# The last token group of a fused attention and feed-forward kernel: 256 tokens, computed and stored token-major

## The chip, the cores and the metric

The kernel runs on one core of one Trainium2 chip. The metric is the device time of one execution in microseconds. A core has five engines with a queue of instructions each: TensorE (PE, with its weight loads as PEld) multiplies matrices into the accumulator memory PSUM; ScalarE (ACT) evaluates functions such as tanh; VectorE (DVE) does elementwise work, reductions and 32x32 block transposes; GpSimd (POOL) and SyncE (SP) do little here but issue DMAs. Each queue is worked off in order. An instruction that needs another engine's result waits on a semaphore, and so does everything behind it in its queue. DMAs between the on-chip memory SBUF and device memory are issued from a queue (here SP's, ACT's or POOL's) and carried out by 16 DMA engines.

## The reference

A polynomial attention without softmax gives x, and a two-layer block with the function h - tanh(h) follows. Shapes: batch 4, heads 4, sequence 1088, head dimension 32; so x has 4352 rows (tokens) of 128.

```python
def phi(x):
    a = np.einsum('rd,bhsd->bhsr', S1, x)          # r = 8
    b = np.einsum('rd,bhsd->bhsr', S2, x)
    return np.einsum('bhsi,bhsj->bhsij', a, b).reshape(*x.shape[:-1], r * r)
q_p, k_p = (phi(q), phi(k))
kv = np.einsum('bhsf,bhsd->bhfd', k_p, v)
z = np.sum(k_p, axis=2)
num = np.einsum('bhsf,bhfd->bhsd', q_p, kv)
den = np.einsum('bhsf,bhf->bhs', q_p, z)[..., None] + 1e-06
attn = num / den
x = np.ascontiguousarray(attn.transpose(0, 2, 1, 3)).reshape(4352, 128)
h = x @ w_in                                        # 128 -> 2048
g = h - np.tanh(h)
out = (g @ w_out).astype(np.float32)                # 2048 -> 128
```

## The kernel before

The kernel is written as a list of operations. Each names its engine or engines, what it reads and writes, an estimated cost and a sort key (`P.add`, L102); `schedule` (L139) places them on the engines by these estimates, `sync` (L268) puts in the semaphores, and `emit` (L316) writes each engine's queue. Buffers come from pools (`_Pool`, `_Val`): an operation that takes a buffer again waits for those that used it last.

Attention leaves its result as `xT` in bfloat16, with the 128 features on the partitions and the tokens as columns. The columns of one batch are ordered by `s = t * 34 + c` with c slow and t fast (NC = 34 blocks of 32 columns): 32 neighbouring columns of `xT` are 32 tokens that lie 34 rows apart in the output, and four blocks of 32 are four neighbouring rows at each t.

The feed-forward part, `ffn(gi, c0, n_)` from L966, works on groups of columns; `GCOLS` (L19) has their sizes, and the last two of the ten have 512 and 192. For each group:

- Sixteen matmuls (L986) make h: for each slice jb of 128 of the 2048 hidden units, the slice of w_in is stationary and the group's columns of xT are moving. They go to PSUM banks of the pool `bank_h` (tiles psh and psa).
- ACT's tanh (L991) takes a unit of m slices at a time from PSUM to a bfloat16 tile `th`; in the last three groups (`gi >= WIDE`, 7) m is 2, or 4 for a group of at most 256 columns; in the first group it is 2, otherwise 1.
- Eighteen matmuls (L1001, L1005) accumulate the output in one bank of the pool `bank_o` (pso or psa): sixteen with a slice of w_out stationary and th moving, and two with a precomputed product of the two weight matrices (`wch` and its rounding rest `wcl`), which supply the linear part h @ w_out. tanh is taken of -h, so that all add up. The result has the 128 outputs on the partitions and the tokens as columns.
- One DVE transpose of 32x32 blocks (L1010) brings it to a tile `ot`: then each group of 32 partitions holds 32 of the 128 outputs, with t on the partitions and (c, m) along the row.
- Four stores (L1020), one for each group of 32 outputs, write `ot` to the output in rows of 32 floats (128 bytes). A group that crosses a batch boundary has eight. They are all issued from SP, except that in the last group two of the four go to ACT's queue. `ot` has three buffers.

At the very end POOL waits for all stores (L1069).

The order around the change: PE's queue interleaves the h matmuls of a unit with the output matmuls of an earlier unit, and the h matmuls of the last group begin while the group before is still being accumulated. On ACT nothing but tanh stands behind the last copies of attention (L378), until the two stores at the end.

Of the kernel before, what the change touches and what calls it, by code (L numbers as in the profile page):

```python
# [4 lines left out]
B, H, S, D = 4, 4, 1088, 32  # L5
R = 8
DM = 128
DFF = 2048
NJB = DFF // 128
NC = 34  # L10
# [5 lines left out]
AF = mybir.ActivationFunctionType  # L16
AX = mybir.AxisListType

GCOLS = [256, 384, 448] + [512] * 6 + [192]  # L19
T_FIRST = 12500.0  # L20
VLAND = [9900.0, 10500.0, 6800.0, 8000.0]
QLAND = [8000.0, 10200.0]
# [306 lines left out]
def _vp(n):  # L329
    return {"vector": (n / 0.96 + 76.0, 158.0)}  # L330


def _a(n):
    return {"scalar": (n * 0.8333 + 50.0, 175.0)}
# [10 lines left out]
def _pe(ns):  # L345
    return {"tensor": (ns, 215.0)}


def bass_polysketch_attn__then__act_tanh_shrink_kernel(
# [10 lines left out]
    P = _Prog()  # L360
    uid = [0]

    def sb(name, shape, dtype=FP32):
        uid[0] += 1
        return nc.alloc_sbuf_tensor(f"{name}_{uid[0]}", shape, dtype).ap()

    def ps(name, n=1):
        uid[0] += 1
        return nc.alloc_psum_tensor(f"{name}_{uid[0]}", [128, n * 512], FP32).ap()
# [4 lines left out]
    def pool(name, n, shape, dtype=FP32):  # L374
        return _Pool([sb(name, shape, dtype) for _ in range(n)])

    def copy(e, name, o, i):
        return e.copy(o, i) if name == "scalar" else e.tensor_copy(o, i)  # L378

    def slices(pl, parts):  # L380
        pl.slots = [[t[:, c:c + w], 0.0, [], (t, c, w)] for (t, c, w) in parts]
        return pl
# [3 lines left out]
    bank_h = slices(_Pool([], True), [(psh, i * 512, 512) for i in range(4)] + [(psa, i * 512, 512) for i in range(2)])  # L386
    bank_o = _Pool([ps("pso"), psa[:, 1024:1536]], True)
# [29 lines left out]
    ot_p = pool("ot", 3, [128, 512])  # L417
    xT = sb("xT", [128, B * S], BF16)
# [12 lines left out]
    wob = sb("wo", [128, NJB, DM], BF16)  # L431
# [3 lines left out]
    woh = [_Val(ap=wob[:, i * 8:(i + 1) * 8, :]) for i in range(2)]  # L435
# [7 lines left out]
                                          start=True, stop=True) for w in (128, 256)], zop, bank_o)  # L443

    def pool_op(fn, r=(), w=(), n=100, key=-50000.0):
        return P.add(_g(n), fn, r=r, w=w, key=key)
# [3 lines left out]
        out=ident.ap[:, :], in_=ident.ap[:, :], pattern=[[-1, 128]], compare_op=ALU.not_equal,  # L450
# [3 lines left out]
        out=mask4.ap[:, :], in_=ident.ap.rearrange("p (q h j) -> p h q j", q=4, h=4), op=ALU.add, axis=AX.XY),  # L454
        r=[ident], w=[mask4], key=-90000)
    P.add(_v(128), lambda e, n: e.tensor_reduce(
        out=mask1.ap[:, :], in_=ident.ap.rearrange("p (h d) -> p h d", h=H), op=ALU.add, axis=AX.X),
        r=[ident], w=[mask1], key=-92000)
    P.add(_v(128), lambda e, n: e.tensor_reduce(
        out=mask2.ap[:, :], in_=ident.ap.rearrange("p (a e d) -> p e a d", a=2, e=2), op=ALU.add, axis=AX.XY),  # L460
        r=[ident], w=[mask2], key=-91000)
    for pl, f, val in ((kT_p, lambda a: a[:, 1088:1152], 0.0), 
                       (m_p, lambda a: a[:, :, 8:9], 1e-6)):
        for i, s_ in enumerate(pl.slots):
            o = pool_op(lambda e, n, a=f(s_[0]), val=val: e.memset(a, val), n=64, key=-49000)
# [82 lines left out]
    gstart = []  # L548
    t = T_FIRST
    for i, gc in enumerate(GCOLS):  # L550
        gstart.append(t)
        t += PERIOD * gc / 512.0

    def col_time(c):
        a = 0
        for i, gc in enumerate(GCOLS):
            if c < a + gc:
# [6 lines left out]
        r=[sqv], w=[stt], key=-85000)  # L564
    P.add(_g(64, 2.2), lambda e, n: e.tensor_tensor(
        out=wq3s.ap.rearrange("p h (x i) -> p h x i", i=8),
        in0=tt[:, None, :, :].to_broadcast([128, H, 2, 8]),
        in1=mask1.ap[:, :, None, None].to_broadcast([128, H, 2, 8]), op=ALU.mult),
        r=[stt, mask1], w=[wq3s], key=-47000)
    P.add(_v(32), lambda e, n: e.tensor_tensor(  # L570
        out=wab.ap.rearrange("p (x e i) -> p x e i", e=2, x=2),
        in0=tt[:, :, None, :].to_broadcast([128, 2, 2, 8]),
        in1=mask2.ap[:, None, :, None].to_broadcast([128, 2, 2, 8]), op=ALU.mult),
        r=[stt, mask2], w=[wab], key=-85000)
    for w, z in zip(wqc, wqs):
# [3 lines left out]
            r=[stt], w=[w], n=16, key=-48000)  # L579
    P.add(_g(128, 2.2), lambda e, n: e.tensor_tensor(  # L580
        out=s2r.ap.rearrange("p (h d) -> p h d", h=H),
        in0=sq[:, 1, None, :].to_broadcast([128, H, 32]),
        in1=mask4.ap[:, :, None].to_broadcast([128, H, 32]), op=ALU.mult),
        r=[sqv, mask4], w=[s2r], key=-70000)

    xvals = []
    seq = [0]
# [348 lines left out]
    def weights():  # L936
# [19 lines left out]
        for jb in range(16):  # L956
# [6 lines left out]
        P.add(_vp(128), lambda e, n: e.tensor_tensor(out=wcl.ap[:, :], in0=wc.ap[:, 0:128], in1=wch.ap[:, :],  # L963
                                                     op=ALU.subtract), r=[wc, wch], w=[wcl], key=-60000.0, name="wcl")

    def ffn(gi, c0, n_):  # L966
        t0 = gstart[gi]
        step = PERIOD / 16 * n_ / 512
        xs = [xv for (a, z, xv) in xvals if a < c0 + n_ and z > c0]
        xt = xT[:, c0:c0 + n_]  # L970
        ov = _Val(bank_o)
        ths = []
        wide = gi >= WIDE
        m = 4 if wide and n_ <= 256 else 2 if wide or n_ <= 256 else 1
        per = 2 if n_ <= 256 else 1
        pitch = 256 if n_ <= 256 else 512
        for j0 in range(0, NJB, m):
            hv = _Val(bank_h, n=m // per)
            th = _Val(th_p, n=-(-m * n_ // 512))
            for j in range(m):  # L980
                jb = j0 + j
                ths.append((th, j * n_))

                def mm(e, n, jb=jb, j=j, hv=hv):
                    c = j % per * pitch
                    return e.matmul(hv.bank(j // per)[:, c:c + n_], wib[:, jb * 128:(jb + 1) * 128], xt, start=True, stop=True)  # L986
                P.add(_pe(n_ / 2.4 + 2.6), mm, r=[wih[jb // 4]] + xs, w=[hv], key=t0 + jb * step, mode="128x128", name=f"h{gi}.{jb}")

            def tanh(e, n, hv=hv, th=th):
                i = hv.ap.rearrange("p (j x) -> p j x", x=pitch)[:, :, 0:n_]  # L990
                return e.activation(out=th.ap[:, 0:m * n_].rearrange("p (j x) -> p j x", x=n_), in_=i, func=AF.Tanh, scale=-1.0)  # L991
            P.add({"scalar": (m * n_ * 0.8333 + 64.0, 175.0)}, tanh,
                  r=[hv], w=[th], key=t0 + (j0 + m - 1) * step, name=f"th{gi}.{j0}")
        seq = [("t", j) for j in range(NJB)]
        at = 15 if gi < 2 else 8
        seq[at:at] = [("c", wch), ("c", wcl)]
        prev = None
        for i, (kind, x) in enumerate(seq):
            st, sp_ = i == 0, i == len(seq) - 1
            if kind == "t":  # L1000
                fn = lambda e, n, x=x, st=st, sp_=sp_: e.matmul(  # L1001
                    ov.ap[:, 0:n_], wob[:, x, :], ths[x][0].ap[:, ths[x][1]:ths[x][1] + n_], start=st, stop=sp_)
                rd = [woh[x // 8], ths[x][0]]
            else:
                fn = lambda e, n, x=x, st=st, sp_=sp_: e.matmul(  # L1005
                    ov.ap[:, 0:n_], x.ap[:, :], xt, start=st, stop=sp_)
                rd = [x] + xs
            prev = P.add(_pe(n_ / 2.4 + 2.6), fn, r=rd, w=[ov], key=t0 + i * step + 1500, chain=prev, mode="128x128", name=f"o{gi}.{i}")
        ot = _Val(ot_p)
        P.add(_vp(n_), lambda e, n: e.transpose(ot.ap[:, 0:n_], ov.ap[:, 0:n_]), r=[ov], w=[ot], key=-60000, name=f"ot{gi}")  # L1010
        cb = c0 // 32
        ce = (c0 + n_) // 32
        while cb < ce:
            b = cb // NC
            cn = min(ce, (b + 1) * NC)
            off = cb * 32 - c0
            for qd in range(4):
                dst = out[b * S:(b + 1) * S, :].rearrange("(t c) m -> t c m", c=NC)[:, cb - b * NC:cn - b * NC, qd * 32:(qd + 1) * 32]
                last = gi == len(GCOLS) - 1
                P.add({"scalar" if last and qd % 2 else "sync": (450.0, 0.0)}, lambda e, n, qd=qd, dst=dst, off=off, w_=(cn - cb) * 32: e.dma_start(  # L1020
                    out=dst, in_=ot.ap[qd * 32:(qd + 1) * 32, off:off + w_].rearrange("p (c m) -> p c m", m=32)),
                    r=[ot], key=t0, dma=(cn - cb) * 32 * 128 / 150.0)
            cb = cn
# [3 lines left out]
    st = {}  # L1027
    for name in ORDER.split():
        b = int(name[1])
# [6 lines left out]
    c = 0  # L1036
    for gi, gc in enumerate(GCOLS):
        ffn(gi, c, gc)
        c += gc
# [75 lines left out]
```

## Time and profile before

| | us |
|---|---|
| median of 13 runs | 108.51 |
| lowest and highest of them | 108.0 and 109.85 |
| the profiled execution, its own time | 108.58 |
| its span in the trace | 106.6 |
| ACT busy in the span | 83.5 (78%) |
| DVE busy | 67.3 (63%) |
| tanh (L991) for 10 groups: 114 and 10 instructions, by the tile they read | 63.2 and 8.6 |
| mean duration of a tanh of 1024 columns from psh (11 of them) | 1.064 |
| mean duration of a tanh of 768 columns from psh (3) | 0.811 |
| output stores: 46 issued from SP, 2 from ACT | |

The span runs from the first to the last instruction in the trace; the execution's own time is 2.0 us longer. The mean durations of matmuls and tanhs include their pipeline's latency, so consecutive ones overlap, and sums of them are no times; the distance between two starts is the cost of one in a row. A view of the profile gives for each row a start or a count, a length, the engine (PE, PEld, DVE, ACT; SPq and ACTq are DMA issues from that queue), the line of the kernel and the tiles as out<-in, and in brackets the idle time before it with what ended it.

### The profile page before, as it was taken

How to read it: one execution, taken by the hardware profiler on the slowest of the kernel's cores; microseconds unless marked ns; L12 is line 12 of the kernel's file. 1: busy time of each engine (PE TensorE's matmuls, PEld its weight loads, DVE VectorE, ACT ScalarE, POOL GpSimd, SP SyncE). 2: the span in 40 equal slices, each digit the busy share in tenths (PEclk: the TensorE clock that was granted, in tenths of full speed). 3: DMA queues.
4: the chain of work that ended last, by engine and by line, in shares of the span. 5: the costliest groups of instructions: out<-in, count | busy, mean ns of one | idle time of the engine just before them, and what ended most of it. 6: DMA issues, size and time to landing. Idle time of an engine off the chain costs nothing.

```text
span 106.6 us, 3421 instructions
## 1 busy us (share of the span) xinstructions
PE 99.2 (93%) x1455; PEld 51.2 (48%) x1455; DVE 67.3 (63%) x114; ACT 83.5 (78%) x174; POOL 5.0 (5%) x23
## 2 busy tenths in 40 slices
PE   5977799899999999999999999999999999999960
PEld 4544688476654356543346343344533444334730
DVE  4569949997965999999999980999420020020210
ACT  0400499997758888788898979999989999999950
POOL 5410320000000000000000000000000000000000
PEclk9999999999999999999999999999999999999997
DMA  2989799966169654015940240033003214014153
GB/s 52 231 249 249 237 118 273 281 188 158 60 152 259 174 104 74 0 22 122 251 122 0 39 66 0 0 53 52 0 3 53 43 31 74 0 16 71 15 79 56
DMA packets 26430, 10.73 MB, mean 101 GB/s; under 512 B 21152, under 2 KB 24240, under 8 KB 26416
## 3 DMA queue, kind: packets, MB, share of 16 engines
q1 hardware_dynamic: 22368, 8.69, 35.5%
q0 software_dynamic: 2112, 0.54, 5.1%
q10 hardware_dynamic: 1936, 1.29, 4.7%
q8 instruction: 11, 0.18, 0.7%
q14 instruction: 3, 0.02, 0.1%
HBM read 8.81 MB, written 2.23 MB: 104 GB/s over the span
## 4 chain that ended last, share of the span: by engine, by line
PE 40%; ACT 31%; DVE 13%; DMA 10%; issue 2%; SPq 1%; DVEq 0%
ACT th L991 27%; PE pso L1001 12%; PE psh L986 9%; DMA vL<-in_v_dram 7%; PE psa L871 7%; DMA sq<-in_S_dram 3%; ACT xT L378 3%; DVE w L735 3%; PE psa L765 2%; DVE abc L812 2%; DVE qp L855 2%; PE psh L671 1%; DVE ot L1010 1%; PE pso L1005 1%; PE psa L804 1%
## 5 line engine op out<-in xcount | busy, mean ns | idle before, releaser
L991 ACT ACTIVATE th<-psh 128x512 bf16<-128x512 f32 (+4 forms) x114 | 63.2, 651 | 3.0 <-PE psh L986 2.8
L986 PE MATMUL psh<-xT,wi 128*128 128x512 bf16 (+4 forms) x142 | 44.0, 347 | 0.1
L1001 PE MATMUL pso<-th,wo 128*128 128x512 bf16 (+3 forms) x128 | 40.3, 358 | 0.3
L1001 PEld LDWEIGHTS pso<-th,wo 128*128 128x128 bf16 x128 | 11.7, 97 | 16.3 <-ACT th L991 4.3
L986 PEld LDWEIGHTS psh<-xT,wi 128*128 128x128 bf16 x142 | 13.4, 98 | 11.4 <-ACT th L991 1.1
L1010 DVE STREAM_TRANSPOSE ot<-pso 128x512 f32<-128x512 f32 (+3 forms) x8 | 5.2, 644 | 15.7 <-PE pso L1001 15.7
L860 DVE STREAM_TRANSPOSE qpT<-qp 128x768 f32<-128x768 f32 (+1 forms) x14 | 12.1, 861 | 0.4
L735 DVE TENSOR_TENSOR w<-abk 128x768 f32<-128x768 f32 (+2 forms) x12 | 11.0, 946 | 0.1
L855 DVE TENSOR_TENSOR qp<-ap,abc 128x768 f32<-128x768 f32 (+1 forms) x13 | 10.7, 825 | 0.1
L871 PE MATMUL psa<-qpT,kvb 32*32 32x128 f32 (+4 forms) x336 | 8.5, 309 | 0.2 <-issue 0.2
L991 ACT ACTIVATE th<-psa 128x1024 bf16<-128x1024 f32 (+2 forms) x10 | 8.6, 908 | 0.0
L442 PE MATMUL pso<-zz 128*128 128x256 bf16 (+1 forms) x41 | 7.4, 337 | 1.1 <-DVE zz L441 1.1
L871 PE MATMUL psh<-qpT,kvb 32*32 32x128 f32 (+4 forms) x112 | 8.5, 310 | 0.0
L1001 PE MATMUL psa<-th,wo 128*128 128x512 bf16 (+1 forms) x32 | 7.4, 314 | 0.3 <-ACT th L991 0.2
L871 PEld LDWEIGHTS psa<-qpT,kvb 32*32 32x32 f32 x336 | 5.1, 103 | 3.6 <-DVE qpT L860 1.2
L1010 DVE STREAM_TRANSPOSE ot<-psa 128x512 f32<-128x512 f32 (+1 forms) x2 | 1.1, 550 | 8.6 <-PE psa L1001 8.6
L442 PEld LDWEIGHTS pso<-zz 128*128 128x128 bf16 x41 | 4.5, 122 | 2.8 <-DVE zz L441 1.1
L986 PE MATMUL psa<-xT,wi 128*128 128x512 bf16 (+1 forms) x18 | 5.6, 349 | 0.0
L615 DVE STREAM_TRANSPOSE qT<-qL 128x576 f32<-128x576 f32 (+3 forms) x8 | 5.4, 706 | 0.0
L809 DVE STREAM_TRANSPOSE abc<-psh 128x288 f32<-128x288 f32 x3 | 1.4, 482 | 5.1 <-PE psh L804 5.0
L703 ACT ACT_TABLE_LOAD x1 | 1.3, 1283 | 4.2 <-issue 4.2
L1001 PEld LDWEIGHTS psa<-th,wo 128*128 128x128 bf16 x32 | 2.6, 97 | 3.6 <-ACT th L991 3.0
(87 smaller groups left out, 96.6 us busy)
## 6 DMA issues: line engine op xcount, KB each, us to landing
vL<-in_v_dram SPq DMA_DIRECT2D x11, 144.0 KB, 3.9
wif<-in_moe_w_in_dram SPq DMA_DIRECT2D x4, 256.0 KB, 6.0
out_dram<-ot SPq DMA_DIRECT2D x16, 64.0 KB, 2.0
kL<-in_k_dram SPq DMA_DIRECT2D x3, 288.0 KB, 3.2
qL<-in_q_dram SPq DMA_DIRECT2D x3, 288.0 KB, 3.8
kL<-in_k_dram SPq DMA_DIRECT2D x3, 256.0 KB, 3.9
qL<-in_q_dram SPq DMA_DIRECT2D x3, 256.0 KB, 3.9
wo<-in_moe_w_out_dram POOLq DMA_DIRECT2D x2, 256.0 KB, 5.7
```

Source lines behind the costliest of these rows:

```text
L378: return e.copy(o, i) if name == "scalar" else e.tensor_copy(o, i)
L442: filler = ([lambda e, n, w=w: e.matmul(bank_o.slots[0][0][:, 0:w], zz.ap[:, 0:128], zz.ap[:, 128:128 + w], start=True, stop=True) for w i ...
L615: P.add(_v((z - a) * 32), lambda e, n: e.transpose(qTs[b][:, a * 32:z * 32], val.ap), r=[val], w=tvs, key=nk(), name=f"qT{b}.{i}")
L735: P.add(_v(nx * 64), lambda e, n: e.tensor_tensor(out=wv.ap[:, 0:nx * 64].rearrange("p (x i j) -> p x i j", i=8, j=8), in0=abh(0)[:, :, :, ...
L765: i = e.matmul(bk[2].ap[h * 32:(h + 1) * 32, 0:64], vL[b][:, h, blk * 32:(blk + 1) * 32], wvs[b, p].ap[:, (bi * 4 + h) * 64:(bi * 4 + h + ...
L855: P.add(_v(cn * 256), lambda e, n, qp=qp, c0=c0, cn=cn: e.tensor_tensor(out=qp.ap[:, 0:cn * 256].rearrange("p (x i j) -> p x i j", i=8, j= ...
L860: P.add(_v(cn * 256), lambda e, n, qp=qp, o0=o0, cn=cn: e.transpose(qt.ap[:, o0 * 256:(o0 + cn) * 256], qp.ap[:, 0:cn * 256]), r=[qp], w=[ ...
L871: i = e.matmul(banks[g].ap[h * 32:(h + 1) * 32, 0:nb * 32], kvb.ap[g * 32:(g + 1) * 32, x, h * 32:(h + 1) * 32], qq[g * 32:(g + 1) * 32, 0 ...
L986: return e.matmul(hv.bank(j // per)[:, c:c + n_], wib[:, jb * 128:(jb + 1) * 128], xt, start=True, stop=True)
L991: return e.activation(out=th.ap[:, 0:m * n_].rearrange("p (j x) -> p j x", x=n_), in_=i, func=AF.Tanh, scale=-1.0)
L1001: fn = lambda e, n, x=x, st=st, sp_=sp_: e.matmul(ov.ap[:, 0:n_], wob[:, x, :], ths[x][0].ap[:, ths[x][1]:ths[x][1] + n_], start=st, stop=sp_)
L1010: P.add(_vp(n_), lambda e, n: e.transpose(ot.ap[:, 0:n_], ov.ap[:, 0:n_]), r=[ov], w=[ot], key=-60000, name=f"ot{gi}")
```

## The change

The last two groups become 448 and 256 instead of 512 and 192. The group of 256 is computed with the operands swapped: for each of its two tiles of 128 tokens, the tile's columns of th (or of xT) are stationary and the slice of w_out (or wch, wcl) is moving, so that the result has the tokens on the partitions and the 128 outputs along the row. Each tile has its own PSUM bank, one from `bank_o` and one from `bank_h`; the two are accumulated alternately, with 36 matmuls of 128 columns in all. The sixteen slices are put through tanh in units of 4, 4, 4, 2 and 2. In place of the transpose there are two plain copies, the first tile's on DVE and the second's on ACT, and in place of the four stores there are two, the first tile's issued from SP and the second's from ACT. Each store writes 128 rows of 512 bytes; its destination runs over (c, t, m) with sizes 4, 32, 128, and its source is 128 partitions of 128 floats.

```diff
-GCOLS = [256, 384, 448] + [512] * 6 + [192]
+GCOLS = [256, 384, 448] + [512] * 5 + [448, 256]
...
+    def token_out(gi, c0, n_, seq, ths, xs, step):
+        b, cl = c0 // S, c0 % S // 32
+        dst = out[b * S:(b + 1) * S, :].rearrange("(t c) m -> c t m", c=NC)
+        prev = None
+        for ti, a in enumerate(range(0, n_, 128)):
+            w_ = min(128, n_ - a)
+            ov = _Val(bank_h if ti else bank_o)
+            for i, (kind, x) in enumerate(seq):
+                st, sp_ = i == 0, i == len(seq) - 1
+                if kind == "t":
+                    lhs, o_, rhs, rd = ths[x][0], ths[x][1] + a, wob[:, x, :], [woh[x // 8], ths[x][0]]
+                else:
+                    lhs, o_, rhs, rd = None, c0 + a, x.ap[:, :], [x] + xs
+                prev = P.add(_pe(56), lambda e, n, lhs=lhs, o_=o_, rhs=rhs, st=st, sp_=sp_, ov=ov, w_=w_: e.matmul(
+                    ov.ap[0:w_, 0:DM], (xT if lhs is None else lhs.ap)[:, o_:o_ + w_], rhs, start=st, stop=sp_),
+                    r=rd, w=[ov], key=gstart[gi] + i * step + 1500 + ti, chain=prev if i else None, mode="128x128", name=f"o{gi}.{ti}.{i}")
+            ot = _Val(ot_p)
+            P.add(_a(DM) if ti else _vp(DM), lambda e, n, ov=ov, ot=ot, w_=w_: copy(e, n, ot.ap[0:w_, 0:DM], ov.ap[0:w_, 0:DM]),
+                  r=[ov], w=[ot], key=-60000, name=f"ot{gi}.{ti}")
+            P.add({"scalar" if ti else "sync": (450.0, 0.0)}, lambda e, n, ot=ot, w_=w_, a=a: e.dma_start(
+                out=dst[cl + a // 32:cl + (a + w_) // 32, :, :], in_=ot.ap[0:w_, 0:DM]),
+                r=[ot], key=gstart[gi], dma=w_ * 512 / 200.0)
...
     def ffn(gi, c0, n_):
...
         m = 4 if wide and n_ <= 256 else 2 if wide or n_ <= 256 else 1
+        units = [(j0, m) for j0 in range(0, NJB, m)]
+        if gi == len(GCOLS) - 1:
+            units[-1:] = [(12, 2), (14, 2)]
         per = 2 if n_ <= 256 else 1
         pitch = 256 if n_ <= 256 else 512
-        for j0 in range(0, NJB, m):
+        for j0, m in units:
...
         seq[at:at] = [("c", wch), ("c", wcl)]
+        if gi == len(GCOLS) - 1:
+            token_out(gi, c0, n_, seq, ths, xs, step)
+            return
...
-                last = gi == len(GCOLS) - 1
-                P.add({"scalar" if last and qd % 2 else "sync": (450.0, 0.0)}, lambda e, n, qd=qd, dst=dst, off=off, w_=(cn - cb) * 32: e.dma_start(
+                P.add({"sync": (450.0, 0.0)}, lambda e, n, qd=qd, dst=dst, off=off, w_=(cn - cb) * 32: e.dma_start(
```

In PE's queue the last group's output matmuls come in blocks: eight behind the first unit's tanh, then the last h matmul of the third unit and the two of the fourth, eight behind the second tanh, four with wch and wcl around the two h matmuls of the fifth unit, eight behind the third tanh, four behind the fourth and four behind the fifth. All instructions of groups 0 to 7 keep their order on every engine.

More of the change, by code (lines that the diff above doesn't have):

```diff
@@ L987, in ffn, with tanh @@
                 P.add(_pe(n_ / 2.4 + 2.6), mm, r=[wih[jb // 4]] + xs, w=[hv], key=t0 + jb * step, mode="128x128", name=f"h{gi}.{jb}")
-            def tanh(e, n, hv=hv, th=th):
+            def tanh(e, n, hv=hv, th=th, m=m):
                 i = hv.ap.rearrange("p (j x) -> p j x", x=pitch)[:, :, 0:n_]
```

## The prediction

> **What bounds the kernel now.** I read the page first, then the chain of waits over the last 20 us, then the timeline of the last 5 us, then the DMA answers. In the page, ScalarE (ACT) is busy for nine tenths or more of nearly every slice at the end, and VectorE (DVE) is almost idle there:
>
> ```profile
> span 106.6 us, 3421 instructions
> ...
> DVE  4569949997965999999999980999420020020210
> ACT  0400499997758888788898979999989999999950
> ```
>
> The chain of waits from 88 us on (start, length, what) shows what sets the end:
>
> ```profile
> 87.56 15.03 ACT th L991 x17
> 102.58 0.05 issue
> 102.63 0.52 PE psa L1001 x4
> 103.15 0.02 issue
> 103.17 0.38 DVE ot L1010
> ```
>
> One unbroken run of tanh ends at 102.58; what follows is a serial tail. The timeline from 102.5 us on (start, length, engine, instruction) has the tail's stores as well:
>
> ```profile
> 101.77 0.81 ACT L991 ACTIVATE th<-psh 128x768 bf16<-128x768 f32 x1
> 102.18 2.21 SPq L1020 DMA_DIRECT2D out_dram<-ot  x4
> 102.63 0.28 PEld L1001 LDWEIGHTS psa<-th,wo 128*128 128x128 bf16 x4 [0.42 <-ACT th L991]
> 102.63 0.50 PE L1001 MATMUL psa<-th,wo 128*128 128x192 bf16 x4 [0.20 <-ACT th L991]
> 103.17 0.38 DVE L1010 STREAM_TRANSPOSE ot<-psa 128x192 f32<-128x192 f32 x1 [1.91 <-PE psa L1001]
> 103.59 0.87 ACTq L1020 DMA_DIRECT2D out_dram<-ot  x2
> ```
>
> The last two stores of each queue are issued one after the other: SP's at 103.58 and 103.94, ACT's at 103.59 and 104.00. Asked for line L1020 in short windows, the trace gives 1.5 and 1.6 us to landing for SP's and 1.7 and 1.8 us for ACT's. The last lands at 104.00 + 1.77 = 105.77, and 0.80 us of closing work leads to 106.57, the span. So the tail after the last tanh is 0.60 (matmuls) + 0.38 + 0.03 (transpose, hand-over) + 0.41 (first issue) + 1.77 (second store) + 0.80.
>
> Two rates are needed. The DMA answer for 2.4 to 2.7 us is a stretch with nothing but 512-byte packets; the one for 60.45 to 60.85 us has 128-byte packets of output stores alone (packets, MB, time that they took as a share of 16 engines):
>
> ```profile
> DMA packets 192, 0.10 MB, mean 325 GB/s; under 512 B 2, under 2 KB 192, under 8 KB 192
> ## 3 DMA queue, kind: packets, MB, share of 16 engines
> q10 hardware_dynamic: 191, 0.10, 106.9%
> ```
>
> ```profile
> DMA packets 410, 0.05 MB, mean 131 GB/s; under 512 B 410, under 2 KB 410, under 8 KB 410
> ## 3 DMA queue, kind: packets, MB, share of 16 engines
> q1 hardware_dynamic: 410, 0.05, 87.3%
> ```
>
> First: 0.3 us x 16 / 191 = 25 ns of one engine for each 512-byte packet (each took 1.069 x 25 = 27). Second: 0.4 x 16 / 410 = 15.6 ns for each 128-byte store packet (each took 13.6). The landings fit "1.3 us + packets on one engine x spacing": SP's first last store has 192 packets, 12 on each of 16 engines, 1.3 + 12 x 0.0156 = 1.49 (measured 1.50); ACT's, 5 ns later, shares the engines with it, 1.3 + 24 x 0.0156 = 1.67 (measured 1.69).
>
> **What the Trainium skill says.** "DMA: Bandwidth & Descriptors", section "Why a DMA increments its semaphore by 16 and not by 1": a DMA issued from SP or ACT uses k engines, the largest k up to 16 that divides the slowest non-1 dimension of both its sides, and these are the lowest-numbered k. Every DMA of the kernel before has 16, 32 or 128 there, so its trace can't test this. The new stores' source is 128 partitions, but their destination is [4 columns c, 32 t, 128 m]: slowest dimension 4, hence k = 4, and the same four engines for both queues. "Issuing engines are not separate DMA queues" there says that DMAs of both queues interleave on the same engines; the 1.50 against 1.69 above agrees. "TensorE: Matmul & The Clock Gate", section "Back-to-back issue gap", gives 81 ns for each matmul in a stream of weight load and 128-column matmul pairs. The trace disagrees: the 16 such pairs of L957 take 1.07 us in all, 0.22 for one alone, so (1.07 - 0.22) / 15 = 57 ns. I take 57.
>
> **The change part by part.**
>
> *Tanh.* Groups 0 to 7 stay as they are, instruction for instruction. For the last two groups ACT had 8 of 1024 and 4 of 768 elements; it gets 8 of 896, 3 of 1024 and 2 of 512: 11264 elements both times, one instruction more. Starts of consecutive tanhs without a stall are 0.90 to 0.92 us apart at 1024 and 0.70 at 768, so 0.8 ns an element and about 0.07 us fixed: +0.07.
>
> *TensorE.* In the old tail a tanh waits for its matmuls three times: gaps of 1.04 (92.98 to 94.02), 0.98 (96.76 to 97.74) and 0.81 (100.26 to 101.06) instead of 0.91, 0.91 and 0.70, 0.31 us together. I walked the new order of both queues with 0.19 us for a 448-column matmul, 0.109 for 256 (both on the line through 0.2155 at 512 and 0.082 at 192, starts in the timeline) and 0.057 for the 36 new ones. They come to 2.05 us instead of 18 x 0.082 = 1.48; the 34 matmuls of the group before lose 34 x 0.027 = 0.92. ACT then waits some 0.05 us at the start of the last group and 0.1 at its third tanh, whose last matmul stands behind eight of the new ones: 0.15 instead of 0.31. Last tanh ends at 102.58 + 0.07 - 0.16 = 102.5 (bounds -0.15 and +0.15).
>
> *Last matmuls.* Two weight slices times two token tiles, 0.05 + 3 x 0.057 + 0.22 + 0.04 = 0.48 to the ACT copy, 0.42 to the DVE copy; before 0.60.
>
> *Copies for the transpose.* No plain DVE copy of 128 columns from PSUM is in the trace; wcl (L963, a subtraction of that size) takes 0.28, a 128-column transpose (L657) 0.29: I take 0.28. The ACT copy like wch (L962, 128x128): 0.265. The ACT copy carries eight waits on group 7's stores and DVE's four on group 6's, since the output buffers go round; the last of group 7's lands at 99.3, so none stalls. Their decoding stands behind the last tanh on ACT and is done while it runs and PE finishes; nothing else is queued behind it but ACT's own store. Cost 0; if that cover failed, 0.1 us for each pair of waits. Group 8's four stores are issued from about 100.3 to 102.1, so SP is free at the end (before, it came free only at 103.23).
>
> *Issues.* One for each queue instead of two: SP at 102.5 + 0.42 + 0.28 + 0.03 = 103.23, ACT at 102.5 + 0.48 + 0.265 + 0.035 = 103.28. The second issue, 0.41, is gone. So far 0.72 us are gained on the last issue.
>
> *Landing.* 256 packets of 512 bytes, in place of 768 of 128. On four engines each gets 64: 64 x 0.026 = 1.66 us, so 103.23 + 1.3 + 1.66 = 106.19. On sixteen it would be 16 x 0.026 = 0.42, so 103.28 + 1.3 + 0.42 = 105.0. A spacing for 512-byte stores isn't in the trace; loads give 25 and 27, the 128-byte stores run 15% above their packets' own time (15.6 on 13.6), which would make 31. Bounds 20 and 36; I take 26.
>
> *Sum, likeliest.* 106.19 + 0.80 = 106.99 against 106.57: +0.42. The profiled execution took 108.58, the median is 108.51; put on the median, 108.9 us. The gain of 0.72 up to the last issue is given back, and more, by stores that use a quarter of the engines.
>
> **The rivals.**
>
> *Spread over 16 engines* (20%). If the split is by source partitions, 105.0 + 0.8 = 105.8, -0.77: 107.7 us. For it: every DMA of the trace so far spreads. Against: none has a short outer dimension.
>
> *Slower by a mechanism of its own* (25%): four engines, and store packets slower than loads. The end is 105.33 + 64 x spacing; it equals the old one at 19.4 ns and is 0.5% later from 27.8 ns on. At 31 ns +0.74, 109.3; at 36 ns +1.06, 109.6. For it: the 15% above. Against: the 512-byte loads run at less than their own 27.
>
> *New matmuls at 81 ns* (5%): the third tanh waits 0.2 us longer and each block of eight pushes the next; 0.4 us in the walk, 109.3 on four engines. Against: L957.
>
> **How the numbers follow.** Likeliest (50%): 108.9, own range 108.4 to 109.2. About 0.5%, 0.54 us, is what a measurement of this kernel can tell from no change. Faster by more: most of the 20% case, 0.19. Slower by more: the two slow cases and a part of the likeliest's upper end, which lies near the threshold, 0.40. Within: 0.41. The range reaches from the 16-engine case to a spacing of 33 ns: 107.7 to 109.4.
>
> **What would show it.** Right: the last tanh ends by 102.6; one store on each queue, issued at 103.2 to 103.3; both landing after 2.6 to 3.1 us; in the DMA answer for the last 2 us a share near a quarter. Wrong: landings of 1.5 to 1.75 us (sixteen engines), a last tanh after 102.8 (matmul spacing), or a span under 106.2.

## The result, and the profile after

The changed kernel took 110.3 us (median of 11 runs, 109.16 to 113.42) beside 108.82 for the kernel before (48 runs): ratio 1.0125, 95% interval 1.0092 to 1.0158, so 1.0 to 1.7 us slower. The ratio leaves out the executions of either kernel that took over 1.5% longer than its fastest. The forecast was 108.9, range 107.7 to 109.4. The profiled execution took 110.32 us, its span is 108.2. The head of the page of the changed kernel:

```profile
span 108.2 us, 3460 instructions
...
DVE  4679939996956999999998962999320010200210
ACT  0400599897668888688895979999899999999920
```

The shape is the old one, but ACT's last slice but one is busy for two tenths, where it was five: the idle end is longer. Not all of the 1.6 us between the two spans comes from the change. The first tanh with 1024 columns starts at 84.61 us before and at 85.27 after, though every instruction ahead of it is the same and stands in the same order. I marked a tanh ahead of the last two groups (the third before that one) in the twelve profiled executions at hand: it starts anywhere between 82.65 and 85.62 us. The four latest are the four where TensorE's granted clock was 0.50 for a stretch between 11 and 19 us; sp_only starts at 84.72 with 3.4 us of that, groups_only at 85.62 with 6.8 us. Neither the kernel before nor the changed one has such a stretch; what makes their marks differ (83.09 and 83.76) the traces don't show. So below the end is measured from that mark or from the end of the last tanh. From the mark to the end of the span it is 23.48 us before and 24.47 after: +0.99 us in the trace. The timed difference can be that or more.

Next, the chain of waits of the changed kernel over the last 20 us (start, length, what):

```profile
87.31 15.09 ACT th L1017 x18
102.39 0.04 issue
...
102.55 0.60 ACT th L1017
103.16 0.05 issue
103.20 0.23 PE psa L979
...
103.64 0.27 ACT ot L378
```

and its timeline from the copies on (start, length, engine, instruction, and in brackets the idle time before it):

```profile
103.58 0.29 DVE L378 COPY ot<-psa 128x128 f32<-128x128 f32 x1 [2.67 <-PE psa L979]
103.64 0.27 ACT L378 COPY ot<-psh 128x128 f32<-128x128 f32 x1 [0.49 <-PE psh L979]
103.90 0.67 SPq L985 DMA_DIRECT2D out_dram<-ot  x1
103.93 1.35 ACTq L985 DMA_DIRECT2D out_dram<-ot  x1
```

Up to here everything is as planned. The tanh run is unbroken, the last tanh ends at 103.15, and the only store of ACT is issued 0.78 us later, where ACT's second store used to follow after 1.42 (SP's after 1.37). The time is lost behind that point. The two issues take 0.67 and 1.35 us, where before they took 0.32 to 0.46. In the trace's semaphore events SP's store lands 2.67 us after its issue and ACT's 3.50, at 107.43; before, the slowest took 1.77. Then the old 0.80 us follow. The sum from the last tanh is 0.78 + 3.50 + 0.80 = 5.08 us, before 1.42 + 1.77 + 0.80 = 3.99: +1.09, less 0.1 that the change had gained ahead of it.

What the transfers do, the DMA answers for the changed kernel show, first for 105.2 to 107.0 us, then for 105.25 to 106.05 and for 106.2 to 106.9 (the first line gives the busy share of 16 engines in tenths for 40 slices; the queue lines packets, MB, share):

```profile
DMA  2212223323233234123222223323323233232510
...
DMA packets 262, 0.14 MB, mean 77 GB/s; under 512 B 8, under 2 KB 261, under 8 KB 261
```

```profile
DMA packets 111, 0.06 MB, mean 71 GB/s; under 512 B 0, under 2 KB 111, under 8 KB 111
## 3 DMA queue, kind: packets, MB, share of 16 engines
q1 hardware_dynamic: 111, 0.06, 27.5%
```

```profile
DMA packets 119, 0.07 MB, mean 96 GB/s; under 512 B 3, under 2 KB 118, under 8 KB 118
## 3 DMA queue, kind: packets, MB, share of 16 engines
q10 hardware_dynamic: 117, 0.06, 27.9%
q14 instruction: 1, 0.01, 2.8%
q1 hardware_dynamic: 1, 0.00, 0.1%
```

For 1.8 us about a quarter of the sixteen engines' time is busy. In the first stretch only SP's packets (q1) move; in the second it is ACT's (q10), beside the last completion write of SP's store and one fetch of instructions (q14). The stores are worked off one behind the other, which fits that they use the same four engines; the trace doesn't name the engine of a packet. The eight packets under 512 bytes are the stores' completion writes, four for each. The semaphore of each store is updated five times: once 1.24 us (SP) and 1.44 us (ACT) after the issue, and four times at the end; every other DMA of the kernel has sixteen updates. "DMA: Bandwidth & Descriptors" in the Trainium skill, section "Why a DMA increments its semaphore by 16 and not by 1", describes this for a DMA on k engines: 16 - k at once, then one for each engine. The trace gives the times of the updates, not their sizes; with one early update and four late ones, k is 4, as forecast.

### The profile page after: what moved, and what is told of

It reads as the page before. It is cut to its first block, busy times and chain, and to the rows that moved or that the text cites. A ratio compares the mean times of both kernels' runs of the same rounds, so it can differ in the third digit from the quotient of the medians.

```text
span 108.2 us, 3460 instructions
## 1 busy us (share of the span) xinstructions
PE 99.4 (92%) x1473; PEld 52.4 (48%) x1473; DVE 67.2 (62%) x114; ACT 83.7 (77%) x176; POOL 5.0 (5%) x23
## 3 DMA queue, kind: packets, MB, share of 16 engines
HBM read 8.81 MB, written 2.23 MB: 102 GB/s over the span
## 4 chain that ended last, share of the span: by engine, by line
PE 43%; ACT 31%; DVE 11%; DMA 9%; issue 1%; SPq 1%; ACTq 0%
ACT th L1017 27%; PE pso L1030 12%; PE psh L1012 10%; DMA vL<-in_v_dram 7%; PE psa L871 7%; DMA sq<-in_S_dram 3%; ACT xT L378 3%; DVE w L735 2%; PE psa L765 2%; PE psa L750 2%; DVE abc L812 2%; PE psh L671 1%; PE pso L1034 1%; PE psa L804 1%; PE psa L782 1%
## 5 line engine op out<-in xcount | busy, mean ns | idle before, releaser
L1012 PE MATMUL psh<-xT,wi 128*128 128x512 bf16 (+3 forms) x140 | 43.7, 349 | 0.1
L1030 PE MATMUL pso<-th,wo 128*128 128x512 bf16 (+3 forms) x128 | 39.8, 354 | 0.3
L1017 ACT ACTIVATE th<-psa 128x512 bf16<-128x512 f32 (+2 forms) x11 | 9.2, 881 | 0.0
L1012 PE MATMUL psa<-xT,wi 128*128 128x512 bf16 (+2 forms) x20 | 5.9, 339 | 0.0
L1030 PE MATMUL psa<-th,wo 128*128 128x512 bf16 x16 | 5.4, 380 | 0.0
L1039 DVE STREAM_TRANSPOSE ot<-psa 128x512 f32<-128x512 f32 x1 | 0.7, 716 | 6.8 <-PE psa L1030 6.8
L378 ACT CAST xT<-psa 128x64 bf16<-128x64 f32 (+4 forms) x11 | 4.3, 436 | 0.0
```

Of the source, the lines that this page charges most:

```text
L1030: fn = lambda e, n, x=x, st=st, sp_=sp_: e.matmul(ov.ap[:, 0:n_], wob[:, x, :], ths[x][0].ap[:, ths[x][1]:ths[x][1] + n_], start=st, stop=sp_)
```

## The experiments

The end of each kernel, in us, from its profiled execution (landing from the semaphore events; the last column is the sum of the three before it up to rounding; sp_only has one store; sp_only, both_on_sp and scratch_rows were executed once):

| kernel | last tanh ends, from the mark | last store issued, after that tanh | it lands, after its issue | to the end of the span | last tanh to the end |
|---|---|---|---|---|---|
| before | 19.49 | 1.42 | 1.77 | 0.80 | 3.99 |
| changed | 19.39 | 0.78 | 3.50 | 0.80 | 5.08 |
| changed_again | 19.38 | 0.78 | 3.50 | 0.80 | 5.08 |
| sp_only | 19.38 | 0.75 | 2.53 | 0.80 | 4.09 |
| both_on_sp | 19.38 | 1.48 | 2.60 | 0.80 | 4.88 |
| tmajor_moving | 19.39 | 0.78 | 2.23 | 0.80 | 3.81 |
| two_c_rows | 19.38 | 0.81 | 2.25 | 0.80 | 3.86 |
| scratch_rows | 19.39 | 0.78 | 1.79 | 0.80 | 3.38 |
| four_stores | 19.38 | 2.29 | 2.18 | 0.96 | 5.43 |
| tmajor | 24.76 | 0.99 | 2.19 | 0.80 | 3.98 |
| tmajor_moving_2 | 19.38 | 0.79 | 2.23 | 0.80 | 3.82 |
| groups_only | 19.50 | 1.60 | 1.88 | 0.80 | 4.27 |

**One queue alone.** If the loss is the two stores' sharing of four engines, half of it goes with one of them; if it is the shape of each store, it stays.

```diff
+            if ti:
+                continue
             P.add({"scalar" if ti else "sync": (450.0, 0.0)}, ...
```

> The changed kernel without ACT's store: the second tile of 128 tokens is computed and copied but not written. If SP's store is slowed by ACT's through the shared engines alone, it lands 1.3 + 32 x 0.025 = 2.1 us after issue (2.67 with ACT's beside it) and its issue takes 0.32 us (0.67 with it). If a store on four engines has its own longer start, it stays at 2.6 us and 0.67.

This kernel leaves the second tile's rows unwritten. The single store's issue took 0.67 us and it landed after 2.53, with five updates of its semaphore. 32 packets on each engine at 26 ns are 0.83; the rest, 1.7 us, is more than the "1.3 us" that the forecast's sum had. The first packet came 1.27 us after the issue, as in the changed kernel. So a second cost exists in one store by itself, beside the four engines.

**Both stores on SP.** ACT's issue of 1.35 us looks like the culprit: is it?

```diff
-            P.add({"scalar" if ti else "sync": (450.0, 0.0)}, ...
+            P.add({"sync": (450.0, 0.0)}, ...
```

> The changed kernel with both stores issued from SP. If the second store starts late because its 32 packets for each of the four engines stand behind the first's, its packets still begin when the first's end and it lands about 3.4 us after the first issue. If it was the clash of two queues (ACT's issue of 1.35 us), the second issue takes 0.67 us and it lands earlier than that.

The issues took 0.67 and 0.55, and the end came 0.20 us earlier than with two queues (4.88 against 5.08). So the long issue on ACT costs at most that 0.20 us; that it was a wait behind SP's store fits, and isn't shown. Here a second queue brought nothing.

**Sixteen engines, by the order of the tokens.** The destination's slowest dimension becomes the 32 steps t when each tile has its tokens in t-major order. First I let the tanh write them so (VectorE makes a copy of xT in the same order for the matmuls with wch and wcl; that part of the edit isn't printed):

```diff
-        dst = ....rearrange("(t c) m -> c t m", c=NC)
+        dst = ....rearrange("(t c) m -> t c m", c=NC)
...
+                if gi == len(GCOLS) - 1:
+                    return e.activation(out=th.ap[:, 0:m * n_].rearrange("p (x t c) -> p x c t", t=32, c=4), ...
```

> Inside each 128-token tile the tokens are put in the order t slow, c fast (the last group's tanh writes its output so, and a copy of xT on VectorE does the same for the two linear matmuls), so each store's destination runs over (t 32, c 4, m 128) in place of (4, 32, 128); sizes, packets, queues and matmuls stay. Theory E (the outer dimension of 4 puts a store on four engines): 16 engines now, SP's store lands 1.5 us and ACT's 1.7 us after issue (after: 2.67 and 3.50), both semaphores rise 16 times, ACT's issue takes 0.4 us (after: 1.35), and the time is 0.5 to 0.8 us below the kernel before. Rival Q (two stores of 128 rows of 512 bytes on two queues are slow in themselves): landings stay at 2.5 us and more, the time stays 1 us above before. Rival M (the loss lies ahead of the stores): landings fall but the time stays above before.

Much slower, ratio 1.0461 (1.042 to 1.0502), and not at the stores. ACT's timeline of tmajor, where L1022 is the tanh that writes every fourth element and L1024 the usual one:

```profile
97.35 1.01 ACT L1024 ACTIVATE th<-psh 128x896 bf16<-128x896 f32 x1
98.28 2.44 ACT L1022 ACTIVATE th<-psh 128x1024 bf16<-128x1024 f32 x1
100.46 2.54 ACT L1022 ACTIVATE th<-psa 128x1024 bf16<-128x1024 f32 x1
102.73 3.68 ACT L1022 ACTIVATE th<-psh 128x1024 bf16<-128x1024 f32 x2
106.15 1.40 ACT L1022 ACTIVATE th<-psa 128x512 bf16<-128x512 f32 x1
```

From start to start a tanh of 1024 takes 2.2 us in place of 0.92. What differs is the output's pattern, runs of 32 columns at a stride of four elements; which of the two, short runs or stride, costs the time was not separated. The stores themselves were issued in 0.62 and 0.65 us and landed after 2.01 and 2.19: the end is shorter, the five tanhs ahead of it cost 5.4 us.

**The same with the order made once.** VectorE, idle at that time, copies xT's 256 columns into t-major order; the h matmuls of the last group and those with wch and wcl read the copy, and tanh stays as it was.

```diff
+        if gi == len(GCOLS) - 1:
+            xp, xw = sbv("xp", [128, n_], BF16), xt
+            P.add(_v(n_), lambda e, n: e.tensor_copy(
+                xp.ap.rearrange("p (a t c) -> p a c t", a=n_ // 128, c=4),
+                xw.rearrange("p (a c t) -> p a c t", a=n_ // 128, c=4)), ...
+            xs, xt = [xp], xp.ap[:, :]
```

> The order t slow, c fast again, but made without strided writes on ScalarE: VectorE copies the group's 256 columns of xT into that order once, and the h matmuls and the linear ones read the copy, so tanh reads and writes contiguous rows. If the strided bfloat16 writes alone made the earlier variant's tanh slow (2.2 us in place of 0.92 for 1024), the last group's tanhs are back at 0.92 and 0.49. Stores: theory E plus S (sixteen engines, but a store whose two sides have different shapes, 128 against 32x4, takes 0.65 us to issue, as the load of S1 does at the start of every run, and starts later): landings 2.0 and 2.2 us after issue, against the kernel before -0.2 to -0.4 us, 1.0 to 1.4 us faster than the changed kernel. If landings of 2.0 there came from the slow tanh's surroundings, they are 1.5 and 1.7 and the gain is 0.7 us.

Its stores (engine, count, issue in ns), the landings, and the DMA answer for 103.9 to 104.9 us:

```profile
L985 SPq DMA_DIRECT2D out_dram<-ot x1: 625/625/625, 102.8 to 102.8; - x1
L985 ACTq DMA_DIRECT2D out_dram<-ot x1: 644/644/644, 102.8 to 102.8; - x1
...
DMA to landing us min/median/max: 2.0/2.1/2.2
```

```profile
DMA  0000000547989998657788998996421000000000
...
DMA packets 288, 0.13 MB, mean 131 GB/s; under 512 B 32, under 2 KB 288, under 8 KB 288
```

Now 32 completion writes stand among the packets, sixteen for each store, and the same 256 rows are through in 0.6 us at up to nine tenths of all engines. From the last tanh it is 3.81 us: 1.27 us less than the changed kernel, with the same bytes, packets and queues. The order of the rows changed along with the number of engines, but a packet takes about as long in both orders: by these shares some 28 ns here, 27 and 32 in the two stretches of the changed kernel. What is gone is that each engine has 64 of them to carry. And yet each issue still takes 0.63 or 0.64 us and SP's first packet comes 1.28 us after it, where the kernel before has 0.32 to 0.46 for an issue.

**Rows to a plain block.** What remains may be the scattered rows or the difference between the two sides' shapes: the source is 128 partitions of 128, the destination 32 x 4 x 128. This kernel is tmajor_moving with both stores into a scratch tensor of 256 rows, shape 128 x 128 for each and on both sides; the last 256 rows of the output stay unwritten.

```diff
-                out=dst[:, cl + a // 32:cl + (a + w_) // 32, :], in_=ot.ap[0:w_, 0:DM]),
+                out=scr[a:a + w_, :], in_=ot.ap[0:w_, 0:DM]),
```

> As the run before it, but the two stores go to a scratch tensor of 256 rows of 128 (the last 256 tokens of the output are left out), so both sides of each store are 128 rows of 512 bytes: same bytes, same rows, same queues, equal shapes. Theory S: issues of 0.32 and 0.38 us, landings of 1.5 and 1.7 us. Rival (128 partitions or 512-byte rows make it slow): 0.62 to 0.67 and 2.0 to 2.2 as with 32x4.

```profile
L986 SPq DMA_DIRECT2D scr<-ot x1: 345/345/345, 103.7 to 103.7; - x1
L986 ACTq DMA_DIRECT2D scr<-ot x1: 354/354/354, 103.7 to 103.7; - x1
...
DMA to landing us min/median/max: 1.7/1.7/1.8
```

Issues of 0.35 us and landings 0.34 and 0.44 us sooner; SP's first packet came 0.85 us after the issue. So 0.43 us belong to the destination of three dimensions against a source of two, or to its scattered rows; four_stores below separates these.

**Rows of 1 KB.** Is that cost one for each row? Here the tiles take the even and the odd columns c, so two neighbouring c lie side by side in the row of a token's partition, and each store has 64 rows of 1024 bytes.

```diff
+                out=dst[16 * h:16 * h + 16, cl:cl + 8, :].rearrange("t (c a) m -> t c (a m)", a=2),
+                in_=ot.ap[64 * h:64 * h + 64, 0:2 * DM]),
```

> As tmajor_moving, but tile 0 takes the even and tile 1 the odd of the eight blocks c, both are copied into one output buffer, and each queue stores 64 partitions of 256 floats: 64 packets of 1 KB for a store in place of 128 of 512 bytes, destination (t 16, c pair 4, 256) on sixteen engines. If the longer issue of a store with sides of different shapes goes with its number of rows (0.65 us at 128 rows against 0.35 with equal shapes), it takes 0.5 us, the landing 1.85 and 2.0 us, and the end is 0.1 to 0.2 us earlier than with tmajor_moving, 0.4 us below the kernel before. If it is a fixed cost of such a store, issue and landing stay at 0.65 and 2.0 to 2.2 us and the time is the same as tmajor_moving's.

Issues of 0.59 and 0.63 us, landings of 2.00 and 2.25: half the rows, twice as long, at the same cost (to 0.04 us in the issues). So it isn't paid by the row.

**Equal shapes without the new order.** The changed kernel, with each store cut into four of one column c: 32 partitions to 32 rows, so both sides are 32 x 128.

```diff
-            P.add({"scalar" if ti else "sync": (450.0, 0.0)}, ...
-                out=dst[cl + a // 32:cl + (a + w_) // 32, :, :], in_=ot.ap[0:w_, 0:DM]),
+            for u in range(w_ // 32):
+                P.add({"scalar" if ti else "sync": (450.0, 0.0)}, ...
+                    out=dst[cl + a // 32 + u, :, :], in_=ot.ap[u * 32:(u + 1) * 32, 0:DM]),
```

> The changed kernel with each tile's store cut into four, one for each c: 32 partitions and a destination (t 32, m 128), four issues on SP and four on ACT. Theory E: each uses 16 engines, 2 packets on each; the fourth issue comes 3 x 0.45 us after the first and lands 1.35 us later: last landing 2.7 us after the first issue in place of 3.5, so 0.7 us faster than the changed kernel, +0.3 us against before. Q: the same bytes on the same two queues, no faster than the changed kernel (+1.3 us).

The first store of each queue had what equal shapes give, though its rows are scattered: issues of 0.33 and 0.37, landings of 1.40 and 1.55, sixteen engines. So scattering isn't the cost, and the difference of the two shapes is left. But eight issues in two rows take until 105.30, 2.29 us after the last tanh, and the third and fourth store of each queue landed only after 2.2 to 2.4 us. Of the sixteen updates of SP's third, fifteen came from 105.95 to 106.11 and the last at 106.96; the other three late ones likewise lack only one engine, for 0.65 to 0.77 us. The DMA answer for 105.6 to 106.2 us has a foreign packet in that stretch:

```profile
q1 hardware_dynamic: 76, 0.02, 19.2%
q10 hardware_dynamic: 45, 0.02, 13.0%
q14 instruction: 1, 0.01, 5.9%
```

5.9% of 16 x 0.6 us is 0.57 us of one engine for one 8 KB fetch of instructions. That it held up the one engine on which the stores ended late fits in time, but no run took it away: the cause stays open. Ratio 1.0217 (1.0166 to 1.0267).

**The groups alone.** The kernel before with only the new sizes of the last groups, so with transpose and four stores for 256 tokens.

```diff
-GCOLS = [256, 384, 448] + [512] * 6 + [192]
+GCOLS = [256, 384, 448] + [512] * 5 + [448, 256]
```

> The kernel before with only the group sizes changed (448 and 256 at the end, transpose and four stores as before). My walk of the queues: last tanh ends 0.05 us later at most (one unit of 1024 at the end, no split), the last four matmuls take 0.1 us more, the transpose of 256 columns 0.45 in place of 0.38 us, the stores of 8 rows land 1.75 to 1.9 us after issue: +0.1 to +0.4 us against before. If the loss of the changed kernel came from the group sizes (rival M), +1 us and more.

Ratio 1.0046 (0.9999 to 1.0093); in its profiled execution, whose stretch at half clock lies ahead of the mark, it is 23.77 us from the mark to the end, 0.29 longer than before. That is small and not sure, but it isn't a gain: what tmajor_moving gains comes from the token-major form, not from the sizes.

**The two bounds again.** The changed kernel on another chip, and tmajor_moving a second time.

> The changed kernel once more, beside the others: from the first tanh of the group of 448 on, its trace is 1.0 us longer than that of the kernel before again; SP's store lands 2.67 and ACT's 3.5 us after issue, ACT's issue takes 1.35 us; the time is +1.0 to +1.5 us against before.

> tmajor_moving once more, in the same call as two_c_rows: issues of 0.62 and 0.64 us, landings of 2.0 and 2.2 us, from the end of the last tanh to the end of the span 3.8 us (before 4.0, changed kernel 5.1), 0.2 to 0.3 us below the kernel before.

changed_again: ratio 1.0105 (1.0051 to 1.016), landings of 2.70 and 3.50. tmajor_moving: 0.9973 (0.9945 to 1.0002) and 0.9973 (0.9946 to 1.0), with landings of 2.01 and 2.23 the second time. two_c_rows gave 0.9976 (0.995 to 1.0003). These two forms are the fastest of those that write the whole output; tmajor_moving's 0.9973 beside changed_again's 1.0105, measured together, puts it 1.3% below the changed kernel. Against the kernel before, 0.3% is at the edge of what these runs can tell.

## Why the prediction was wrong

Its steps, against the trace:

- *Tanh and TensorE's stalls*: the last tanh was to end 0.08 us earlier than before; it ends 0.09 earlier from the mark. Right. ACT's waits for matmuls in the last two groups came to about 0.2 us instead of 0.31; the walk had 0.15. Of the new matmuls, consecutive starts lie 0.056 us apart (57 ns taken); the rival of 81 ns fell.
- *Last matmuls, copies, issues*: 0.42 and 0.48 us to the copies, measured 0.43 and 0.49; copies of 0.28 and 0.265, measured 0.29 and 0.27; issues 0.73 and 0.78 us after the last tanh, measured 0.75 and 0.78. Right, and so was the 0.72 us gained on the last issue: 0.09 by the earlier tanh and 0.64 after it (1.42 became 0.78). The eight waits on ACT's copy cost nothing: the last two tanhs start 0.48 us apart, what 512 columns take.
- *Four engines*: right, by the share of about a quarter, the five updates and the eight completion writes. The rival of sixteen engines fell for this kernel, and tmajor_moving shows that it was also priced too well: from the mark sixteen engines gain 0.27 us, not 0.77. That the packets of both queues interleave, as the prediction had it, doesn't show here: the second store's began as the first's ended, where those of the last stores before overlapped by about half (104.58 to 104.73 us, of 0.33 us each). For the sum it makes no difference.
- *Landing, the step that failed*: "1.3 us + packets on one engine x spacing" gave 1.3 + 64 x 0.026 = 2.96 us from SP's issue to the last landing. Measured: 103.90 to 107.43, 3.53. Of the missing 0.57, the first term has most: the packets began 1.27 us after the issue, where a store of equal shapes takes 0.85 (scratch_rows), so +0.42. The drain, 105.17 to 106.96 for 64 packets, has 28 ns for each packet, not 26: +0.13. The rival with slow packets (31 and 36 ns) named the smaller part, and 28 lies nearer to 26. The forecast had bounds for the spacing and none for the 1.3.

The 1.3 had been fitted to stores whose two sides are both 32 x columns x 32, and the forecast carried it over to a store with a destination of three dimensions and a source of two. Nothing in the profile backed that. One row of the trace of before hinted at it: the load of S1, an expanded 16 x 8 on one side and 128 partitions on the other. In the answer for line L479 of the kernel before, beside its neighbour:

```profile
L479 SPq DMA_DIRECT2D sq<-in_S_dram x1: 672/672/672, 0.7 to 0.7; - x1
L479 ACTq DMA_DIRECT2D kL<-in_k_dram x1: 443/443/443, 0.7 to 0.7; - x1
```

672 ns is the issue of SP's new store (674) to two nanoseconds. It is a hint and no proof: other loads of that line take 311 to 1222 ns to issue. An operand that is new in shape was to be looked up by shape, and not by direction. With 0.57 more, the sum is +0.99, which is the trace's own difference.

Not all of the distance from 108.9 to 110.3 is the kernel's: the forecast was put on 108.51, and the kernel before had 108.82 in the comparison. The timed difference, 1.36 us at the middle of its interval, leaves 0.37 over. The mean granted clocks of the profiled executions, 0.995 before and 0.988 after, don't explain it. In each page the row of the clock, first before and then after, falls in the last slice alone:

```profile
PEclk9999999999999999999999999999999999999997
PEclk9999999999999999999999999999999999999995
```

In both traces it is 1.00 from 7 us until 105.4 and 105.7 us, and 0.50 from there to the end, 1.1 us before and 2.5 us after. TensorE has nothing left to do by then, so the lower mean comes of the longer end and not the other way round. What the clock does ahead of the end differs between executions: those with a mean of 0.985 or more took 109.7 us with the changed kernel (10, changed_again included) and 108.6 with the kernel before (70), 1.1 apart. So most of the rest comes with executions of lower clock; whether the changed kernel brings more of them no run has settled.

## What to carry to other kernels

A store at the very end of a kernel is priced from both of its access patterns. The slowest dimension counts first: one of 4 gave four engines here, and 16, 32 and 128 gave sixteen; for 128 KB that is 1.27 us. Sides of different shape cost about another 0.43 us, with rows of 512 bytes and of 1 KB alike. Where the order of a dimension is free, make it the one that puts the large factor outermost, and make it on data that is small and early (256 columns of input), not in the tanh that is the bound. And before a fitted formula is carried over, ask whether its terms were fitted on the same kind of object; a search of the old trace for the nearest shape costs a minute.

## What the runs showed of the hardware

- tanh with a bf16 output in runs of 32 at a stride of four elements: 2.18 to 2.27 us for 1024 columns from start to start, 0.92 with a dense output; one of 512 columns lasts 1.40 instead of 0.60.
- Two stores from different queues on four engines did not mix: the second one's packets began at 106.11, as the first one's last began at 106.17, and its issue stretched to 1.35 us (1.37 in the second execution). Whether the packets waited for the issue or for the engines isn't shown. On sixteen engines (tmajor_moving) no issue stretched, but the packets overlapped by no more than 0.07 us either, and by 0.26 us with equal shapes (scratch_rows).
- From the start of its last packet to its landing a store took 0.38 to 0.42 us on sixteen engines and 0.35 to 0.47 on four, the late ones of four_stores aside.
